# Turning keys, queries and normalised tiles by the DMA crossbar instead of TensorE, on a queue shared with stores

## The chip, the cores and the metric

One core of one Trainium2 chip. The metric is device microseconds (us) of one execution; a number for a kernel is the median of all its runs, slow ones included, with the lowest and highest beside it. An execution counts as fast or slow by its granted TensorE clock and its time; the ratios and their intervals use fast runs alone. The sets of experiments ran on different chips, each with the kernel before beside it.

## The reference, cut to what matters

Attention in chunks of 32 queries over their own keys, 16 to the left, 8 to the right and 8 memory rows, for 4 batches of 8 heads, 768 tokens, head size 64. Its output x (768 x 512 per batch) is normalised, multiplied by g, and goes through two large products with a ReLU between:

```python
for c in range(nc):                                   # 24 chunks of 32
    k_full = np.concatenate([mem_k, k[:, :, l_start:r_end]], axis=2)
    v_full = np.concatenate([mem_v, v[:, :, l_start:r_end]], axis=2)
    scores = scale * np.matmul(q_c, k_full.transpose(0, 1, 3, 2))
    a = np.exp(scores - max); a = a / (a.sum() + 1e-9)
    out[:, :, c_start:c_end] = np.matmul(a, v_full)
# x = out as (batch, 768, 512)
xn = (x - mu) / np.sqrt(var + 1e-06) * g_ln
return x + np.maximum(xn @ w_ch1, 0.0) @ w_ch2        # 512 -> 2048 -> 512
```

## The kernel before: the parts concerned

24 tiles of 128 tokens are worked in 8 units of three. A unit has 28 steps: 16 of the up-product (`up`, L319), then 12 of the down-product (`down`, L336). A table says at which step what else is put between: attention of the next unit's tiles, loads, and the turning of keys and queries. Every engine and every queue runs its own list in order.

```python
def turn_x(u, i, t, kind="att"):              # a normalised tile, 128 x 512, turned on TensorE
    pv = as16(slot("att")[:, 0, :]) ...
    for dt in range(4):
        nc.tensor.matmul(out=pv[...], lhsT=xn[t % 3][...], rhs=identity, is_transpose=True, ...)   # L296
    nc.scalar.copy(out=xT[u % 2][:, :, 128 * i : 128 * i + 128], in_=...)
# turn_kq (L176): 16 matmuls for a pair of heads of keys or queries; keep_k, keep_q copy them to KT, QZ
def v_around(b):                              # borders between groups of V, SBUF to SBUF, queue SP
    nc.sync.dma_start(out=vt[8:24, 1:NG, :, :], in_=vt[72:88, 0 : NG - 1, :, :])
    nc.sync.dma_start(out=vt[88:96, 0 : NG - 1, :, :], in_=vt[24:32, 1:NG, :, :])
...
elif u in (2, 4):
    attend(((1, 8, 8, 12), (4, 8, 10, 14), (11, 17, 17, 21)))   # scores, values, norm, turn_x of 3 tiles
    for j, step in ((0, 17), (2, 23)):
        at(step, kq_block, b, j, 0, NG, "mm"); at(step, keep_rest)
    for h in range(H):
        at(2 + 2 * h, load_v_head, b, h)
    at(21, mem_cols, b); at(21, v_mem, b); at(22, v_around, b)
elif following:
    attend(((12, 17, 17, 21), (14, 17, 17, 22), (18, 23, 23, 26)))
```

The softmax here doesn't subtract the row's maximum and nothing guards it: scores larger than these inputs give would overflow.

Of the kernel before, what the change touches and what calls it, by code (L numbers as in the profile page):

```python
# [9 lines left out]
FP16 = mybir.dt.float16  # L10
# [5 lines left out]
def kernel(  # L16
# [17 lines left out]
    KR = 96  # L34
    KC = NG * KR + 32
    HD = 65
# [21 lines left out]
    w2c = [sb.tile([128, 4, 512], FP16, name=f"w2c{i}") for i in range(4)]  # L58
    k16 = [sb.tile([96, H, 8, 64], FP16, name=f"k16_{i}") for i in range(2)]
    q16 = [sb.tile([96, H, 8, 64], FP16, name=f"q16_{i}") for i in range(2)]  # L60
    V = [sb.tile([128, NG, H, HD], FP16, name=f"V{i}") for i in range(2)]
    KT = [sb.tile([128, 4, KC], FP16, name=f"KT{i}") for i in range(2)]
    QZ = [sb.tile([128, 4, NG, 2, 64], FP16, name=f"QZ{i}") for i in range(2)]
    AT = [sb.tile([128, 2, H, 64], FP16, name=f"AT{i}") for i in range(3)]
# [45 lines left out]
    def load_v_group(b, g):  # L110

        lo, hi = max(64 * g - 16, 0), min(64 * g + 72, S)
        r = 24 + lo - 64 * g
        nc.gpsimd.dma_start(  # L114
            out=V[b % 2][r : r + hi - lo, g, :, 0:64],
            in_=dram(v, b * H * HS + lo * D, [[64, hi - lo], [HS, H], [1, 64]]),
        )

    def load_v_head(b, h):
        nc.gpsimd.dma_start(  # L120
            out=V[b % 2][24:88, :, h, 0:64],
            in_=dram(v, (b * H + h) * HS, [[64, 64], [64 * 64, NG], [1, 64]]),
        )

    def v_around(b):

        vt = V[b % 2]
        nc.sync.dma_start(out=vt[8:24, 1:NG, :, :], in_=vt[72:88, 0 : NG - 1, :, :])
        nc.sync.dma_start(out=vt[88:96, 0 : NG - 1, :, :], in_=vt[24:32, 1:NG, :, :])

    def v_mem(b):
        src = memv16[:, b, :, :]
        nc.sync.dma_start(
            out=V[b % 2][0:8, :, :, :],
            in_=bass.AP(tensor=src.tensor, offset=src.offset,
                        ap=[list(src.ap[0]), [0, NG], [1, H * HD]]),
        )
# [26 lines left out]
    def mem_cols(b):  # L164
        src = memKT[:, 4 * b : 4 * b + 4, :]
        nc.vector.tensor_copy(
            out=free(KT[b % 2], 0, [[KC, 4], [KR, NG], [1, 8]]),
            in_=bass.AP(tensor=src.tensor, offset=src.offset,
                        ap=[list(src.ap[0]), [8, 4], [0, NG], [1, 8]]),
        )  # L170
# [13 lines left out]
    def keep_k(pv, b, j, n, g0, g1, copy=nc.vector.tensor_copy):  # L184

        for ga, gb in ((0, 1), (1, NG - 1), (NG - 1, NG)):
            ga, gb = max(ga, g0), min(gb, g1)
            if ga < gb:
                lo = 0 if ga == 0 else 8 * ga - 2
                m = 10 if gb == NG else 8 * ga + 9 - lo  # L190
                copy(  # L191
                    out=free(KT[b % 2], j * KC + 24 + 32 * ga + 8 * lo,
                             [[KR, gb - ga], [8, m], [1, 8]]),
                    in_=free(pv, lo, [[8, gb - ga], [1, m], [n, 8]]),
                )

    def keep_q(copy, pv, b, j, par, n, g0, g1):


        rows = slice(64 * par, 64 * par + 64)  # L200
        copy(  # L201
            out=free(QZ[b % 2][rows, j, g0, par, :], 0, [[128, g1 - g0], [8, 8], [1, 8]]),
            in_=free(pv[rows, :], 8 * g0, [[8, g1 - g0], [1, 8], [n, 8]]),
        )
# [24 lines left out]
    def keep_rest():  # L229
        kept_later.pop(0)()  # L230

    def scores(b, t):
        p = slot("att")
        a = AT[t % 3]
        for gg in range(2):
            g = 2 * t + gg
            for j in range(4):
                nc.tensor.matmul(  # L238
                    out=p[:, gg, 128 * j : 128 * j + 128],
                    lhsT=KT[b % 2][:, j, KR * g : KR * g + 128],  # L240
                    rhs=QZ[b % 2][:, j, g, :, :],
                    start=True, stop=True,
                )
# [48 lines left out]

    def turn_x(u, i, t, kind="att"):
        pv = as16(slot("att")[:, 0, :]) if kind == "att" else as16(slot("mm")[:, :])
        for dt in range(4):
# [72 lines left out]
    def clear_k(i):  # L368
        nc.vector.memset(KT[i][:, :, 8:24], 0.0)
        nc.vector.memset(KT[i][:, :, NG * KR - 8 : KC], 0.0)  # L370

# [32 lines left out]
    for h in (0, 4):  # L404
        for which in range(2):
            load_kq(0, which, 0, CUT, h, h + 4)
    keep(counts[:, 0:1], counts[:, 0:1], 24, 0.0)
    keep(counts[:, 1:2], counts[:, 1:2], -88, 0.0)
    make_identity(nc, identity)
# [7 lines left out]
    mem_cols(0)  # L417
    pg = slot("mm")[:, :]
    nc.tensor.matmul(out=pg, lhsT=ones32, rhs=g_one, start=True, stop=True)
    nc.scalar.copy(out=g_row, in_=pg)  # L420
    v_mem(0)
# [5 lines left out]
    nc.gpsimd.memset(zero2[:, 1:2], -NEG)  # L427
    keep(band[:, 0:1], zero2[:, 0:1], -64, NEG)
    keep(band[:, 1:2], zero2[:, 0:1], 40, NEG)
    keep(zero2[:, 1:2], zero2[:, 1:2], -8, 0.0)  # L430
    nc.gpsimd.tensor_tensor(out=band[:, 1:2], in0=band[:, 1:2], in1=zero2[:, 1:2], op=ALU.add)
    for g in range(4, 6):
# [47 lines left out]
    scores(0, 1)  # L480
    stay_busy(5)
    values(0, 0)
# [20 lines left out]
    for u, tiles in enumerate(units):  # L503
# [6 lines left out]

        def attend(steps):

            for i, (s0, s1, s2, s3) in enumerate(steps):
                t = following[i]
                at(s0, scores, t // 6, t % 6)
                at(s1, values, t // 6, t % 6)
                at(s2, norm, t % 6, t % 9)
                at(s3, turn_x, u + 1, i, t % 6)
                at(min(s3 + 1, 27), root, t % 6, t % 9)

        late = ((16, 19, 19, 22), (17, 21, 21, 24), (19, 23, 23, 26))
        if u == 0:
# [10 lines left out]
            for g in range(6):  # L533
                at(15, load_v_group, 1, g)
            attend(late)
            at(26, mem_cols, 1)
            at(26, v_mem, 1)
        elif u == 1:
# [3 lines left out]
            for g in range(6, NG):  # L542
                at(0, load_v_group, 1, g)
            for which in range(2):
                at(1, load_kq, 2, which)
            attend(late)
        elif u in (2, 4):
            attend(((1, 8, 8, 12), (4, 8, 10, 14), (11, 17, 17, 21)))
            b = u // 2 + 1
            for j, step in ((0, 17), (2, 23)):  # L550
                at(step, kq_block, b, j, 0, NG, "mm")
                at(step, keep_rest)
            for h in range(H):
                at(2 + 2 * h, load_v_head, b, h)
            at(21, mem_cols, b)
            at(21, v_mem, b)
            at(22, v_around, b)
        elif following:
            attend(((12, 17, 17, 21), (14, 17, 17, 22), (18, 23, 23, 26)))
            if u == 3:  # L560
                for which in range(2):
                    at(2 + which, load_kq, 3, which)
        for step in range(16 + 4 * n):
# [43 lines left out]
```

## Time and profile before

| | before |
|---|---|
| time, beside the changed kernel's first run | 232.52 us (230.87 to 233.24, 4 runs) |
| span of the profiled run | 230.2 us |
| TensorE busy | 222.8 us, 97% of the span |
| waits of TensorE after 50 us | none listed |
| unit 2, unit 3 | 27.11 us, 24.04 us, TensorE busy throughout |

The lines, and what follows from them, are in the prediction.

### The profile page before, as it was taken

Reading aid. Unit: us, or ns where it says so; the run is one execution under the profiler, and the core shown is the slowest. Engines: PE = TensorE matmul, PEld = TensorE weight load, DVE = VectorE, ACT = ScalarE, POOL = GpSimd, SP = SyncE. Lnnn points to the kernel's source line nnn. Section 1 sums busy time; section 2 is a strip of 40 time slices with the busy share of each in tenths; the row PEclk is TensorE's granted clock in tenths of the full one; section 3 lists DMA queues with packets and bytes.
Section 4 is the critical chain, followed back from the end, with each engine's and each line's share of the span. In section 5 each row is a group of like instructions: output and inputs, shape, how many; then the busy total and the mean of one; then the engine's idle time right before and its main releaser. Section 6 shows DMA issues by size and latency. Waiting matters only on the chain.

```text
span 230.2 us, 5499 instructions
## 1 busy us (share of the span) xinstructions
PE 222.8 (97%) x2289; PEld 138.2 (60%) x2289; DVE 125.4 (54%) x290; ACT 119.0 (52%) x228; POOL 68.6 (30%) x125
## 2 busy tenths in 40 slices
PE   7989999899999999999999999999999999999993
PEld 2455776447765577555765577556765566557553
DVE  5746881475747639575336648674436542663222
ACT  3565648253894576655355367654356335534200
POOL 6973343877360380530001370410001200030000
PEclk9999999999999999999999999999999999999999
DMA  5999999999999999548921199543001200111012
GB/s 80 169 90 203 201 211 150 125 200 226 121 69 126 226 145 36 37 77 119 236 48 48 48 127 23 37 99 106 0 3 46 90 4 0 47 48 46 0 48 93
DMA packets 50307, 21.91 MB, mean 95 GB/s; under 512 B 37817, under 2 KB 46777, under 8 KB 50234
## 3 DMA queue, kind: packets, MB, share of 16 engines
q0 software_dynamic: 45680, 14.23, 90.1%
q1 hardware_dynamic: 4602, 7.33, 10.5%
q8 instruction: 18, 0.29, 0.6%
q14 instruction: 7, 0.06, 0.1%
HBM read 28.48 MB, written 6.29 MB: 151 GB/s over the span
## 4 chain that ended last, share of the span: by engine, by line
PE 77%; DMA 16%; POOL 2%; DVE 2%; issue 1%; POOLq 0%
PE mm L319 32%; PE mm L336 32%; DMA w2c<-in_moe_w_ch_dram 13%; PE att L238 4%; DMA V<-in_v_dram 3%; PE att L258 3%; PE att L176 3%; PE att L296 2%; POOL V L114 2%; PE mm L354 2%; PE mm L176 1%; DVE QZ L374 1%; DVE V L379 0%; DVE V L378 0%; DVE osb L359 0%
## 5 line engine op out<-in xcount | busy, mean ns | idle before, releaser
L319 PE MATMUL mm<-xT,w1c 128*128 128x384 f16 x512 | 88.3, 326 | 0.0
L336 PE MATMUL mm<-w2c,rT 128*128 128x512 f16 x368 | 87.4, 379 | 0.2 <-DMA w2c<-in_moe_w_ch_dram 0.2
L319 PEld LDWEIGHTS <-w1c 128*128 128x128 f16 x512 | 57.0, 114 | 24.2 <-issue 0.3
L327 DVE TENSOR_SCALAR rT<-mm 128x384 f16<-128x384 f32 x64 | 35.5, 556 | 35.3 <-PE mm L319 35.1
L336 PEld LDWEIGHTS <-rT 128*128 128x128 f16 x368 | 33.8, 98 | 34.0 <-issue 0.3
L325 ACT ACTIVATE rT<-mm 128x384 f16<-128x384 f32 x64 | 31.2, 489 | 35.9 <-PE mm L319 33.9
L245 ACT ACTIVATE AT<-att,band 96x512 f16<-96x512 f32 x48 | 30.1, 677 | 17.1 <-PE att L238 16.6
L287 POOL TENSOR_SCALAR veps<-squares 128x1 f32<-128x1 f32 x24 | 4.5, 188 | 109.9 <-ACT junk L284 95.1
L343 DVE SCALAR_TENSOR_TENSOR osb<-mm,rstd,xs 128x512 f32<-128x512 f32 x23 | 17.2, 749 | 30.9 <-PE mm L336 20.4
L114 POOL DMA_DIRECT2D V<-in_v_dram x24 | 21.5, 900 | 15.5 <-DMA V<-in_v_dram 4.5
L301 ACT COPY xT<-att 128x512 f16<-128x512 f16 x21 | 12.2, 581 | 23.8 <-PE att L296 23.8
L191 DVE COPY KT<-att 128x80 f16<-128x80 f16 (+3 forms) x44 | 18.4, 480 | 2.1 <-PE att L176 2.1
L278 DVE SCALAR_TENSOR_TENSOR xn<-xs,nmean,g_row 128x512 f16<-128x512 f32 x24 | 18.0, 752 | 0.9
L201 ACT COPY QZ<-mm 64x768 f16<-64x768 f16 (+1 forms) x18 | 13.6, 757 | 8.0 <-PE mm L176 7.8
L268 DVE RECIPROCAL rec<-att 128x8 f32<-128x8 f32 x24 | 4.9, 203 | 23.3 <-PE att L258 23.3
L284 ACT ACTIVATE junk<-xs,nmean 128x512 f16<-128x512 f32 x24 | 17.4, 724 | 0.1
L269 DVE SCALAR_TENSOR_TENSOR xs<-att,rec 128x512 f32<-128x512 f32 x24 | 16.6, 691 | 0.8
L238 PE MATMUL att<-QZ,KT 128*128 128x128 f16 x192 | 14.8, 219 | 0.9 <-ACT AT L245 0.6
L238 PEld LDWEIGHTS <-KT 128*128 128x128 f16 x192 | 12.6, 98 | 4.6 <-issue 1.4
L201 ACT COPY QZ<-att 64x384 f16<-64x384 f16 (+1 forms) x20 | 12.0, 598 | 5.3 <-PE att L176 5.1
L291 POOL TENSOR_TENSOR rstd<-veps,mhalf 128x1 f32<-128x1 f32 x24 | 13.3, 553 | 2.0
L258 PEld LDWEIGHTS <-AT 96*64 96x64 f16 x384 | 7.9, 111 | 8.7 <-issue 6.0
(63 smaller groups left out, 145.5 us busy)
## 6 DMA issues: line engine op xcount, KB each, us to landing
out_dram<-osb SPq DMA_DIRECT2D x23, 256.0 KB, 5.9
w1c<-in_moe_w_ch_dram POOLq DMA_DIRECT2D x4, 512.0 KB, 12.0
w2c<-in_moe_w_ch_dram POOLq DMA_DIRECT2D x4, 512.0 KB, 15.7
V<-in_v_dram POOLq DMA_DIRECT2D x20, 88.0 KB, 14.1
k<-in_k_dram POOLq DMA_DIRECT2D x2, 768.0 KB, 12.4
q<-in_q_dram POOLq DMA_DIRECT2D x2, 768.0 KB, 16.1
V<-in_v_dram POOLq DMA_DIRECT2D x16, 96.0 KB, 5.9
k<-in_k_dram POOLq DMA_DIRECT2D x3, 256.0 KB, 6.3
```

Source lines behind the costliest of these rows:

```text
L114: nc.gpsimd.dma_start(out=V[b % 2][r : r + hi - lo, g, :, 0:64], in_=dram(v, b * H * HS + lo * D, [[64, hi - lo], [HS, H], [1, 64]]),)
L191: copy(out=free(KT[b % 2], j * KC + 24 + 32 * ga + 8 * lo, [[KR, gb - ga], [8, m], [1, 8]]), in_=free(pv, lo, [[8, gb - ga], [1, m], [n, 8]]),
L201: copy(out=free(QZ[b % 2][rows, j, g0, par, :], 0, [[128, g1 - g0], [8, 8], [1, 8]]), in_=free(pv[rows, :], 8 * g0, [[8, g1 - g0], [1, 8], ...
L238: nc.tensor.matmul(out=p[:, gg, 128 * j : 128 * j + 128], lhsT=KT[b % 2][:, j, KR * g : KR * g + 128], rhs=QZ[b % 2][:, j, g, :, :], start ...
L245: nc.scalar.activation(out=free(a, 32 * c, [[512, 2], [64, 8], [1, 32]], KR), in_=free(p, 32 * c, [[512, 2], [64, 8], [1, 32]], KR), func= ...
L278: nc.vector.scalar_tensor_tensor(out=xn[i], in0=x, scalar=nmean[i], in1=g_row, op0=ALU.add, op1=ALU.mult,)
L284: nc.scalar.activation(out=junk, in_=xs[xi], func=ACTF.Square, bias=nmean[i], accum_out=squares[i],)
L319: nc.tensor.matmul(out=p, lhsT=free(w, i, [[4, 128]]), rhs=xT[u % 2][:, dt, 0 : 128 * n], start=(dt == 0), stop=(dt == 3),)
L325: nc.scalar.activation(out=o, in_=p, func=ACTF.Relu)
L327: nc.vector.tensor_scalar(out=o, in0=p, scalar1=0.0, scalar2=None, op0=ALU.max)
L336: nc.tensor.matmul(out=p, lhsT=rT[hc][:, 128 * i : 128 * i + 128], rhs=w2c[hc // 4][:, hc % 4, :], start=(hc == 0), stop=(hc == 15),)
L343: nc.vector.scalar_tensor_tensor(out=o, in0=p, scalar=rstd[t % 9], in1=xs[t % 9], op0=ALU.mult, op1=ALU.add,)
```

## The change

The intent: take the turning off TensorE. Keys and queries of batches 2 and 3 are loaded token by token and turned by the DMA crossbar in four parts each, fitted between the stores on SP's queue; VectorE spreads the queries over zeros; GpSimd copies the borders between key groups. 17 normalised tiles are turned by the crossbar as well. The product that spreads g over 128 rows moves behind the first scores, and the fillers around it (matmuls on zeros that keep TensorE busy, `stay_busy`) are exchanged. The steps of the attention of units 2 to 6 move too, as the diff shows. The layout of KT, QZ and V changes to suit. Core of the diff:

```diff
+    def load_tokens(b, which, t):              # six of each per batch, 256-byte runs
+        nc.gpsimd.dma_start(out=free(dst, 512 * t, [[64, H], [1, 64]]), in_=dram(src, ...))
+    def cross_k(b, half, t0, t1):
+        nc.sync.dma_start_transpose(out=free(KT[b % 2], ...), in_=kraw[0][64 * half : 64 * half + 64, 512 * t0 : 512 * t1])
+    def cross_q(half, t0, t1): ...             # the same into QT
+    def k_around(b, t0, t1): ...               # 4 GpSimd copies of key borders
+    def spread_q(b, half, t0, t1): ...         # 2 VectorE copies QT -> QZ
     def turn_x(u, i, t, kind="att"):
+        if kind == "dma":
+            nc.sync.dma_start_transpose(out=xT[u % 2][:, :, 128 * i : 128 * i + 128], in_=xn[t % 3])
+            return
...
-            for which in range(2):
-                at(1, load_kq, 2, which)
-            attend(late)
+            for t in range(6):
+                for which in range(2):
+                    at(23, load_tokens, 2, which, t)
+            attend(((16, 19, 19, 19), (17, 19, 20, 20), (21, 23, 23, 26)), "att")
...
+            if u in (3, 5):
+                attend(((10, 15, 15, 15), (12, 15, 16, 16), (17, 21, 21, 21)))
+            else:
+                attend(((9, 14, 14, 14), (11, 14, 15, 15), (16, 20, 20, 20)))
             if u in (2, 4):
-                kq_block ... at steps 17 and 23; v_mem at 21; v_around at 22
+                at(16, cross_k, b, 0, 0, 4)
+                at(20, cross_k, b, 1, 0, 4)
+                at(20, cross_q, 0, 0, 3)
+                at(21, cross_q, 1, 0, 3)
+                at(27, k_around, b, 0, 4)
+            elif u in (3, 5):
+                for half in range(2):
+                    at(6 + half, spread_q, b, half, 0, 3)
+                    at(1, cross_k, b, half, 4, 6)
+                    at(1, cross_q, half, 3, 6)
+                at(4, k_around, b, 4, 6)
+                at(5, v_mem, b)
+                at(5, v_around, b)
+                ... spread_q of the other half at 18 and 19
```

Line numbers move with it: L319 becomes L374, L336 L391, the values product L258 becomes L308; L345 is the crossbar transpose of a tile, L247 and L253 those of keys and queries, L130 and L131 the moves of V's borders, L401 the stores.

More of the change, by code (lines that the diff above doesn't have):

```diff
@@ L34 @@
     KR = 96
-    KC = NG * KR + 32
     HD = 65
@@ L58 @@
     w2c = [sb.tile([128, 4, 512], FP16, name=f"w2c{i}") for i in range(4)]
-    k16 = [sb.tile([96, H, 8, 64], FP16, name=f"k16_{i}") for i in range(2)]
-    q16 = [sb.tile([96, H, 8, 64], FP16, name=f"q16_{i}") for i in range(2)]
+    kraw = [sb.tile([128, 4096], FP16, name=f"kraw{i}") for i in range(2)]
+    qraw = [sb.tile([128, 4096], FP16, name=f"qraw{i}") for i in range(2)]
+    QT = sb.tile([128, NG * 4 * 64], FP16, name="QT")
+    k16 = [t[0:96, 0:4096].rearrange("p (h r d) -> p h r d", h=H, r=8) for t in kraw]
+    q16 = [t[0:96, 0:4096].rearrange("p (h r d) -> p h r d", h=H, r=8) for t in qraw]
     V = [sb.tile([128, NG, H, HD], FP16, name=f"V{i}") for i in range(2)]
-    KT = [sb.tile([128, 4, KC], FP16, name=f"KT{i}") for i in range(2)]
-    QZ = [sb.tile([128, 4, NG, 2, 64], FP16, name=f"QZ{i}") for i in range(2)]
+    KT = [sb.tile([128, NG * 4 * KR + 32], FP16, name=f"KT{i}") for i in range(2)]
+    QZ = [sb.tile([128, NG, 4, 2, 64], FP16, name=f"QZ{i}") for i in range(2)]
     AT = [sb.tile([128, 2, H, 64], FP16, name=f"AT{i}") for i in range(3)]
@@ L112, in load_v_group @@
         lo, hi = max(64 * g - 16, 0), min(64 * g + 72, S)
-        r = 24 + lo - 64 * g
+        r = 16 + lo - 64 * g
         nc.gpsimd.dma_start(
@@ L120, in load_v_head @@
         nc.gpsimd.dma_start(
-            out=V[b % 2][24:88, :, h, 0:64],
+            out=V[b % 2][16:80, :, h, 0:64],
             in_=dram(v, (b * H + h) * HS, [[64, 64], [64 * 64, NG], [1, 64]]),
@@ L127, in v_around @@
         vt = V[b % 2]
-        nc.sync.dma_start(out=vt[8:24, 1:NG, :, :], in_=vt[72:88, 0 : NG - 1, :, :])
-        nc.sync.dma_start(out=vt[88:96, 0 : NG - 1, :, :], in_=vt[24:32, 1:NG, :, :])
+        nc.sync.dma_start(out=vt[0:16, 1:NG, :, :], in_=vt[64:80, 0 : NG - 1, :, :])
+        nc.sync.dma_start(out=vt[80:88, 0 : NG - 1, :, :], in_=vt[16:24, 1:NG, :, :])
     def v_mem(b):
@@ L133, in v_mem @@
         nc.sync.dma_start(
-            out=V[b % 2][0:8, :, :, :],
+            out=V[b % 2][88:96, :, :, :],
             in_=bass.AP(tensor=src.tensor, offset=src.offset,
@@ L166, in mem_cols @@
         nc.vector.tensor_copy(
-            out=free(KT[b % 2], 0, [[KC, 4], [KR, NG], [1, 8]]),
+            out=free(KT[b % 2], KR - 8, [[KR, 4], [4 * KR, NG], [1, 8]]),
             in_=bass.AP(tensor=src.tensor, offset=src.offset,
@@ L191, in keep_k @@
                 copy(
-                    out=free(KT[b % 2], j * KC + 24 + 32 * ga + 8 * lo,
-                             [[KR, gb - ga], [8, m], [1, 8]]),
+                    out=free(KT[b % 2], (4 * ga + j) * KR + 16 + 8 * (lo - 8 * ga),
+                             [[4 * KR, gb - ga], [8, m], [1, 8]]),
                     in_=free(pv, lo, [[8, gb - ga], [1, m], [n, 8]]),
@@ L201, in keep_q @@
         copy(
-            out=free(QZ[b % 2][rows, j, g0, par, :], 0, [[128, g1 - g0], [8, 8], [1, 8]]),
+            out=free(QZ[b % 2][rows, g0, j, par, :], 0, [[512, g1 - g0], [8, 8], [1, 8]]),
             in_=free(pv[rows, :], 8 * g0, [[8, g1 - g0], [1, 8], [n, 8]]),
@@ L230, in keep_rest, with place, cross_q, k_around @@
         kept_later.pop(0)()
+    def place(b, g):
+        return g if b < 2 else g % 2 * (NG // 2) + g // 2
+    def load_tokens(b, which, t):
+        dst, src = ((kraw[0], k), (qraw[0], q))[which]
+        nc.gpsimd.dma_start(
+            out=free(dst, 512 * t, [[64, H], [1, 64]]),
+            in_=dram(src, b * H * HS + 128 * t * D, [[D, 128], [HS, H], [1, 64]]),
+        )
+    def cross_k(b, half, t0, t1):
+        nc.sync.dma_start_transpose(
+            out=free(KT[b % 2], (24 * half + 4 * t0) * KR + 16, [[KR, 4 * (t1 - t0)], [1, 64]]),
+            in_=kraw[0][64 * half : 64 * half + 64, 512 * t0 : 512 * t1],
+        )
+    def cross_q(half, t0, t1):
+        nc.sync.dma_start_transpose(
+            out=free(QT, (24 * half + 4 * t0) * 64, [[64, 4 * (t1 - t0)], [1, 64]]),
+            in_=qraw[0][64 * half : 64 * half + 64, 512 * t0 : 512 * t1],
+        )
+    def k_around(b, t0, t1):
+        kt, a = KT[b % 2], max(t0, 1)
+        own = lambda half, t: (24 * half + 4 * t) * KR
+        for dst, src, m, w in (
+            (own(1, t0), own(0, t0) + 64, t1 - t0, 16),
+            (own(0, a), own(1, a - 1) + 64, t1 - a, 16),
+            (own(0, t0) + 80, own(1, t0) + 16, t1 - t0, 8),
+            (own(1, a - 1) + 80, own(0, a) + 16, t1 - a, 8),
+        ):
+            nc.gpsimd.tensor_copy(
+                out=free(kt, dst, [[KR, 4 * m], [1, w]]), in_=free(kt, src, [[KR, 4 * m], [1, w]])
+            )
+    def spread_q(b, half, t0, t1):
+        for par in range(2):
+            rows = slice(64 * par, 64 * par + 64)
+            nc.vector.tensor_copy(
+                out=QZ[b % 2][rows, 6 * half + t0 : 6 * half + t1, :, par, :],
+                in_=QT[rows, (24 * half + 4 * t0) * 64 : (24 * half + 4 * t1) * 64].rearrange(
+                    "p (t j x) -> p t j x", j=4, x=64),
+            )
     def scores(b, t):
@@ L235, in scores @@
         for gg in range(2):
-            g = 2 * t + gg
+            g = place(b, 2 * t + gg)
             for j in range(4):
@@ L239, in scores @@
                     out=p[:, gg, 128 * j : 128 * j + 128],
-                    lhsT=KT[b % 2][:, j, KR * g : KR * g + 128],
-                    rhs=QZ[b % 2][:, j, g, :, :],
+                    lhsT=KT[b % 2][:, (4 * g + j) * KR : (4 * g + j) * KR + 128],
+                    rhs=QZ[b % 2][:, g, j, :, :],
                     start=True, stop=True,
@@ L293, in turn_x @@
     def turn_x(u, i, t, kind="att"):
+        if kind == "dma":
+            nc.sync.dma_start_transpose(
+                out=xT[u % 2][:, :, 128 * i : 128 * i + 128], in_=xn[t % 3]
+            )
+            return
         pv = as16(slot("att")[:, 0, :]) if kind == "att" else as16(slot("mm")[:, :])
@@ L368, in clear_k @@
     def clear_k(i):
-        nc.vector.memset(KT[i][:, :, 8:24], 0.0)
-        nc.vector.memset(KT[i][:, :, NG * KR - 8 : KC], 0.0)
+        end = 4 * KR * (NG - 1)
+        nc.vector.memset(free(KT[i], 0, [[KR, 4], [1, 16]]), 0.0)
+        nc.vector.memset(free(KT[i], end + 80, [[KR, 4], [1, 8]]), 0.0)
+        nc.vector.memset(KT[i][:, end + 4 * KR : end + 4 * KR + 32], 0.0)
     def clear_q(i, par):
@@ L406 @@
             load_kq(0, which, 0, CUT, h, h + 4)
-    keep(counts[:, 0:1], counts[:, 0:1], 24, 0.0)
-    keep(counts[:, 1:2], counts[:, 1:2], -88, 0.0)
+    keep(counts[:, 0:1], counts[:, 0:1], 16, 0.0)
+    keep(counts[:, 1:2], counts[:, 1:2], -80, 0.0)
     make_identity(nc, identity)
@@ L417 @@
     mem_cols(0)
-    pg = slot("mm")[:, :]
-    nc.tensor.matmul(out=pg, lhsT=ones32, rhs=g_one, start=True, stop=True)
-    nc.scalar.copy(out=g_row, in_=pg)
+    stay_busy(4)
     v_mem(0)
@@ L427 @@
     nc.gpsimd.memset(zero2[:, 1:2], -NEG)
-    keep(band[:, 0:1], zero2[:, 0:1], -64, NEG)
-    keep(band[:, 1:2], zero2[:, 0:1], 40, NEG)
-    keep(zero2[:, 1:2], zero2[:, 1:2], -8, 0.0)
-    nc.gpsimd.tensor_tensor(out=band[:, 1:2], in0=band[:, 1:2], in1=zero2[:, 1:2], op=ALU.add)
+    keep(band[:, 0:1], zero2[:, 0:1], -56, NEG)
+    keep(band[:, 1:2], zero2[:, 0:1], 32, NEG)
+    keep(zero2[:, 1:2], zero2[:, 1:2], 88, 0.0)
+    nc.gpsimd.tensor_tensor(out=band[:, 0:1], in0=band[:, 0:1], in1=zero2[:, 1:2], op=ALU.add)
     for g in range(4, 6):
@@ L480 @@
     scores(0, 1)
-    stay_busy(5)
+    stay_busy(2)
+    pg = slot("mm")[:, :]
+    nc.tensor.matmul(out=pg, lhsT=ones32, rhs=g_one, start=True, stop=True)
+    nc.vector.tensor_copy(out=g_row, in_=pg)
+    stay_busy(1)
     values(0, 0)
@@ L509, in at, with attend @@
             plan.setdefault(step, []).append((fn, args))
-        def attend(steps):
+        def attend(steps, kind="dma"):
             for i, (s0, s1, s2, s3) in enumerate(steps):
@@ L517, in attend @@
                 at(s2, norm, t % 6, t % 9)
-                at(s3, turn_x, u + 1, i, t % 6)
-                at(min(s3 + 1, 27), root, t % 6, t % 9)
-        late = ((16, 19, 19, 22), (17, 21, 21, 24), (19, 23, 23, 26))
+                at(s3, turn_x, u + 1, i, t % 6, kind if i == 2 or u == 0 else "dma")
+                at(min(s3 + 3, 27), root, t % 6, t % 9)
         if u == 0:
@@ L534 @@
                 at(15, load_v_group, 1, g)
-            attend(late)
+            attend(((16, 19, 19, 22), (17, 21, 21, 24), (19, 23, 23, 26)), "att")
             at(26, mem_cols, 1)
@@ L543 @@
                 at(0, load_v_group, 1, g)
-            for which in range(2):
-                at(1, load_kq, 2, which)
-            attend(late)
-        elif u in (2, 4):
-            attend(((1, 8, 8, 12), (4, 8, 10, 14), (11, 17, 17, 21)))
-            b = u // 2 + 1
-            for j, step in ((0, 17), (2, 23)):
-                at(step, kq_block, b, j, 0, NG, "mm")
-                at(step, keep_rest)
-            for h in range(H):
-                at(2 + 2 * h, load_v_head, b, h)
-            at(21, mem_cols, b)
-            at(21, v_mem, b)
-            at(22, v_around, b)
-        elif following:
-            attend(((12, 17, 17, 21), (14, 17, 17, 22), (18, 23, 23, 26)))
+            for t in range(6):
+                for which in range(2):
+                    at(23, load_tokens, 2, which, t)
+            attend(((16, 19, 19, 19), (17, 19, 20, 20), (21, 23, 23, 26)), "att")
+        elif following:
+            if u in (3, 5):
+                attend(((10, 15, 15, 15), (12, 15, 16, 16), (17, 21, 21, 21)))
+            else:
+                attend(((9, 14, 14, 14), (11, 14, 15, 15), (16, 20, 20, 20)))
+            b = u // 2 + 1
+            if u in (2, 4):
+                for h in range(H):
+                    at(2 + 2 * h, load_v_head, b, h)
+                at(16, cross_k, b, 0, 0, 4)
+                at(20, cross_k, b, 1, 0, 4)
+                at(20, cross_q, 0, 0, 3)
+                at(21, cross_q, 1, 0, 3)
+                at(21, mem_cols, b)
+                at(27, k_around, b, 0, 4)
[7 more added lines that the diff above has]
+                at(5, v_around, b)
+                for half in range(2):
+                    at(18 + half, spread_q, b, half, 3, 6)
             if u == 3:
-                for which in range(2):
-                    at(2 + which, load_kq, 3, which)
+                for t in range(6):
+                    for which in range(2):
+                        at(21, load_tokens, 3, which, t)
         for step in range(16 + 4 * n):
```

## The prediction

> **What bounds the kernel now.** I read the page's first two parts, then the waits of TensorE alone, then the chain that ended last, then the groups by shape. First the shares of the span and the slices:
>
> ```profile
> span 230.2 us, 5499 instructions
> PE 222.8 (97%) x2289; PEld 138.2 (60%) x2289; DVE 125.4 (54%) x290; ACT 119.0 (52%) x228; POOL 68.6 (30%) x125
> ...
> PE   7989999899999999999999999999999999999993
> ...
> PEclk9999999999999999999999999999999999999999
> DMA  5999999999999999548921199543001200111012
> ```
>
> TensorE (PE) is busy 97% of the span at the full granted clock; VectorE and ScalarE a little over half. The DMA row matters later: nearly full for the first 16 slices (92 us), then with holes. Asked for TensorE's waits from 50 us on, the trace lists none; in the whole run the waits inside the work (after the start) are at most 0.8 us, the last on a weight transfer at 48.9 us. So from 50 to 226 us each microsecond taken from TensorE is a microsecond of time, as long as nothing makes it wait. The chain says which pieces those are. A stretch of it, columns start, us and what:
>
> ```profile
> 94.63 0.68 PE att L176 x32
> 95.32 0.68 PE mm L176 x32
> 96.00 3.56 PE mm L336 x16
> 99.56 0.22 PE att L296 x4
> 99.78 1.73 PE mm L336 x8
> 101.50 0.80 PE att L176 x32
> 102.31 0.68 PE mm L176 x32
> 102.99 3.56 PE mm L336 x16
> 106.55 8.45 PE mm L319 x52
> ```
>
> L176 turns keys and queries of batch 2 on TensorE (128 small matmuls), L296 turns a normalised tile, L336 and L319 are the two big products. Both kinds of turning are on the chain. The evictions belonging to them:
>
> ```profile
> L201 ACT COPY QZ<-mm 64x768 f16<-64x768 f16 x16 | 12.7, 793 | 7.1 <-PE mm L176 7.0
> L191 DVE COPY KT<-att 128x880 f16<-128x880 f16 x12 | 12.8, 1064 | 0.0
> L301 ACT COPY xT<-att 128x512 f16<-128x512 f16 x21 | 12.2, 581 | 23.8 <-PE att L296 23.8
> out_dram<-osb SPq DMA_DIRECT2D x23, 256.0 KB, 5.9
> memk<-in_mem_k_dram SPq DMA_DIRECT2D x1, 64.0 KB, 1.9
> ```
>
> The first three have idle engines around them and cost no time now. The last two are the only landing times on the queue (SP) that the new transposes will use.
>
> **What the Trainium skill says.** "VectorE: DVE Perf Modes", section "The three transpose paths": 128x128 bf16 takes 390 ns on TensorE and 1309 ns by the DMA crossbar, which writes SBUF directly. The trace shows 219 ns for one L296 matmul, but four in 0.22 us of the chain, that is 55 ns of TensorE time each: pipelined, turning here is far cheaper than the page's single figure, so little is won per tile. "Advanced Engine Details and Errata", section "X-Bar Transpose (TRN2)": transposing DMAs are as fast as ordinary ones; the trace before has none, so it can't say. "VectorE: DVE Perf Modes", section "The TRN2 errata" gives 58 + elements/speed-up cycles at 0.96 GHz for SBUF to SBUF; no such f16 copy of size is in the trace, so I use it for an estimate of the new query copies only.
>
> **The change part by part.**
> 1. Keys and queries of batches 2 and 3 leave TensorE. From the chain: batch 2 loses 0.68 + 0.68 + 0.80 + 0.68 = 2.84 us, batch 3 (at 145.79, 146.47, 152.66, 153.46 us) the same 2.84. Sum 5.68 us, all on the path.
> 2. Normalised tiles turned by DMA: i = 0 and 1 of the unit after u = 1, and all three in u = 2 to 6, 17 tiles of 68 matmuls. Their pieces in the chain are 0.22 us, but for two of 0.35; 15 x 0.22 + 2 x 0.355 = 4.0 us, on the path. The listing of the instructions agrees: TensorE has 644 rows fewer, that is 2 x (256 + 68) less 4 for two more fillers.
> 3. Evictions that go: 16 ScalarE copies of 0.79 us, 17 of 0.58 us, and on VectorE 8 x (1.064 + 0.23 + 0.225) = 12.2 us. None is on the path, so they are worth nothing by themselves; they take away reasons to wait.
> 4. Added on VectorE: 16 copies spreading queries, 64 partitions x 768. Estimate by the skill's formula at four elements a cycle (58 + 192)/0.96 = 0.26 us each, 4 us in all. On GpSimd: 24 loads in place of 4 (about 0.75 us to issue, as the row of the head loads of V, 742 ns median), and 16 copies of key borders. Beside TensorE, with more than a unit between load and use in most places.
> 5. The product with g goes from 5.86 us to behind the first scores, with fillers exchanged. Before, its two passes took 1.36 us and four fillers now stand there; later 5 fillers become 3 and the product. This start is followed by waits for transfers (0.83 us for V at 44 us, 0.18 us for w2 at 48.9 us) that are set by the load queue, which hardly changes. I count 0 for it, half a microsecond either way.
> 6. Layout (memory rows last, groups outermost in KT and QZ): same sizes of matmuls, 0.
>
> Gross: 5.68 + 4.0 = 9.7 us, 4.2%.
>
> **What is given back.** The new dependence is a transposed tile needed whole at the next unit's first product. In units 2, 4 and 6 the last tile's values product is in step 20, so steps 21 to 27 remain, 7 x 0.866 (four L336 matmuls) = 6.1 us. From the end of the values product to xn the timeline of before shows 126.81 to 129.09 = 2.3 us (reciprocal, product, mean, L278). Left for issue, transpose and landing: 3.8 us. In units 3 and 5 step 21 is used, so 5.2 - 2.3 = 2.9 us. What does a 128 KB transpose take? Estimate: between the 64 KB load (1.9 us) and the 256 KB store (5.9 us) by a straight line, 1.9 + 64 x 4.0/192 = 3.2 us. That fits into even units and misses in odd ones by 0.3 to 0.7 us, with issue. In unit 3 the loads of batch 3's tokens run on the same 16 engines just then: I add 1 us. In unit 1 the third tile stays on TensorE, so no wait there. Sum 0.7 x 2 + 1 = about 2.4 us.
>
> Net 9.7 - 2.4 = 7.3 us; 232.9 - 7.3 = 225.6, and I say **225.3 us**.
>
> **The rivals.**
> *A. Nothing is given back.* The crossbar lands in 2 us or so (the skill's 1309 ns and "as fast as regular" point there, and the differing steps 20 and 21 look tuned). Then 232.9 - 9.7 = 223.2 us.
> *B. The tile transpose takes the place of the TensorE one as a wait.* If it lands only after 5.9 us, as the stores do, even units wait 2.1 us and odd ones 3.0: 3 x 2.1 + 2 x 3.0 = 12.3 us, more than the gain, 235.5 us. For it: all 23 stores have such a landing; against it: they write to DRAM and twice the bytes.
> *C. The SP queue is the bound.* Stores and transposes share one in-order queue, where each issue waits for its VectorE result. In units 3 and 5 four key and query transposes, then the fill of V's memory rows and the two moves of V's borders (0.73, 0.57, 1.0 us to issue before) stand in front of the values product of step 15, some 11 us into the unit. If one transpose costs SP 2 us to issue, 1 + 8 + 2.3 + landing 3 = 14 us, and TensorE waits 3 us twice: 229 to 231 us. Nothing in the trace of before measures that issue; the plain ones take 0.33 to 1.0 us, which speaks against 2.
> *D. VectorE or ScalarE becomes the bound.* Both lose more than they get; I give it next to nothing.
>
> **Range and chances.** A gives 223.2, the sum above 225.6, C about 230, B 235.5. I weigh A with 0.3, the sum with 0.4, C with 0.2 and B with 0.1. The 2% line is 228.3 us, beyond which C and B lie in part. Range 222.0 to 230.5 us; faster 0.76, same 0.20, slower 0.04.
>
> **What would show it.** Right: TensorE busy about 213 us, 324 turning matmuls gone from L176 and L296's successors, span near 222.5, no wait of TensorE over 1 us after 50 us except at unit starts, where the up-product waits for the DMA of xT, in units 4 and 6 first (after the odd ones). Step 1 wrong: TensorE's busy time falls by less than 9 us. Landing estimate wrong: transposes of xn landing well under 3 us (A) or near 6 us with a wait at every unit start (B). C: the values product at step 15 waiting for a DMA of V, and SP busy issuing. The prediction fails above all if the transposes, mixed with 256-byte token loads, land late, which would show as waits on DMA of KT, QT or xT.

## The result and the profile after

244.34 us (241.79 to 245.91, 4 runs, one of them slow) against 232.52 us: ratio 1.0482, interval 1.0374 to 1.0591. A ratio here is the mean time of one kernel's fast runs over that of the other's of the same rounds, so not quite the ratio of the medians quoted. The changed kernel is slower, outside the range.

The page's head and slices of the changed kernel:

```profile
span 242.3 us, 4931 instructions
PE 218.3 (90%) x1967; PEld 130.7 (54%) x1967; DVE 122.2 (50%) x285; ACT 98.6 (41%) x194; POOL 91.0 (38%) x161
...
PE   7989999899999999759679699989719999999995
...
PEclk9999999999999999989979999999977999999999
```

TensorE's busy time fell by 4.5 us only, its share to 90%, and there are slices at 1 to 7 tenths (each is 6.06 us) at 97 to 109, 115 to 127, 133 to 139 and 170 to 182 us. The clock row dips below 9 at or behind most of them. The timeline of TensorE names the waits (start, duration, group, and in brackets the idle time before and what ended it):

```profile
105.61 8.99 PE L374 MATMUL mm<-xT,w1c 128*128 128x384 f16 x44 [4.03 <-DMA xT<-xn]
...
122.59 0.71 PE L308 MATMUL att<-V,AT 96*64 96x65 f16 x32 [3.85 <-DMA V<-V]
...
138.44 6.66 PE L374 MATMUL mm<-xT,w1c 128*128 128x384 f16 x40 [2.06 <-DMA xT<-xn]
...
162.98 7.31 PE L374 MATMUL mm<-xT,w1c 128*128 128x384 f16 x44 [1.02 <-DMA xT<-xn]
...
180.95 1.10 PE L308 MATMUL att<-V,AT 96*64 96x65 f16 x32 [6.52 <-DMA V<-V]
```

Those are five waits, 17.5 us: three for a turned tile xT at a unit's start (4.03, 2.06, 1.02 us) and two for the moves of V's borders before the values product of step 15 in units 3 and 5 (3.85 and 6.52 us). No wait for KT or QT.

They cost more than themselves. Windows of the changed kernel, unit by unit: length, then busy TensorE, weight load, VectorE, ScalarE, GpSimd (number of instructions), granted clock, transfer share (the packets' time as a share of the 16 DMA engines'; above 1 where packets overlap), GB/s. Units 3, 5 and 6 do the same work on TensorE:

```profile
105.61:138.44 32.83, 26.92 (x185) 15.13 (x185) 14.69 (x34) 9.81 (x20) 10.75 (x20) 0.90 0.72 105
138.44:162.98 24.54, 23.52 (x185) 14.05 (x185) 12.14 (x27) 9.95 (x20) 12.58 (x21) 1.00 2.90 130
162.98:194.92 31.94, 25.42 (x185) 14.81 (x184) 13.87 (x33) 9.81 (x20) 4.04 (x13) 0.89 0.50 97
194.92:218.28 23.36, 23.36 (x186) 14.04 (x185) 11.86 (x26) 9.95 (x20) 2.21 (x6) 1.00 0.17 52
```

Unit 6, undisturbed, needs 23.36 us of TensorE; unit 3 needed 26.92 and unit 5 25.42 at mean clocks of 0.90 and 0.89. So 3.56 + 2.06 = 5.6 us went into matmuls at a lowered clock: in finer windows the clock reads 0.50 from 107 to 109 us, from 124 to 126 and from 181 to 185, each time shortly after one of the three long waits. The account: -9.7 (work removed) + 17.5 + 5.6 = 13.4, against 242.3 - 230.2 = 12.1; unit 2 began 1.38 us earlier than before, 0.44 us of it being two turned tiles, which the 9.7 already holds. The other 0.94, of which 0.54 came before unit 1 (begun at 51.19 us against 51.73), makes up most of the rest.

What SP's queue did in units 2 and 3 of the changed kernel (start, time held, instruction):

```profile
94.58 3.51 SPq L247 DMA_TRANSPOSE KT<-kraw  x1
...
98.83 3.91 SPq L345 DMA_TRANSPOSE xT<-xn  x1
...
104.27 3.37 SPq L253 DMA_TRANSPOSE QT<-qraw  x2
107.74 1.14 SPq L401 DMA_DIRECT2D out_dram<-osb  x2
108.98 1.93 SPq L247 DMA_TRANSPOSE KT<-kraw  x1
111.08 1.22 SPq L253 DMA_TRANSPOSE QT<-qraw  x1
112.35 1.52 SPq L247 DMA_TRANSPOSE KT<-kraw  x1
113.92 1.29 SPq L253 DMA_TRANSPOSE QT<-qraw  x1
...
116.95 1.06 SPq L131 DMA_DIRECT2D V<-V  x1
```

The third tile's transpose (98.83) held the queue for 3.91 us behind a key transpose. Another key and two query transposes, then two stores whose results VectorE had had ready since 99.1 and 102.4 us (its L398), then four more transposes until 115.21, stand before the moves of V, which were meant for step 5 and were issued at 116.3 to 118.0 us; the values product began at 122.59. And the landing times in the list of transfers:

```profile
out_dram<-osb SPq DMA_DIRECT2D x23, 256.0 KB, 2.3
...
xT<-xn SPq DMA_TRANSPOSE x17, 2.4
...
KT<-kraw SPq DMA_TRANSPOSE x8, 4.2
```

The list gives a tile 2.4 us at the median, sooner than the 3.2 us estimated, but the profile resolves only 3 of the 17 landings, and the tiles that TensorE waited for are mostly not among them. The tile issued at 133.11 us landed 5.28 us later (in the chain), and the wait for the one issued at 98.83 ended at 105.61. Loads were in flight beside both: beside the first the token loads of batch 3, issued from 131.1 us on; beside the second batch 2's eight loads of V, issued at 87.6 to 92.8 us, which landed until 103.6 by the completion events of the trace. The question is what stands before and beside a tile.

### The profile page after: what moved, and what is told of

The parts are those of the page before. It is cut to its first block, busy times and chain, and to the rows that moved or that the text cites. A ratio compares the mean times of both kernels' runs of the same rounds, so it can differ in the third digit from the quotient of the medians.

```text
span 242.3 us, 4931 instructions
## 1 busy us (share of the span) xinstructions
PE 218.3 (90%) x1967; PEld 130.7 (54%) x1967; DVE 122.2 (50%) x285; ACT 98.6 (41%) x194; POOL 91.0 (38%) x161
## 4 chain that ended last, share of the span: by engine, by line
PE 37%; SPq 12%; DMA 11%; POOL 5%; issue 2%; DVE 1%; ACT 0%; DVEq 0%; ACTq 0%; POOLq 0%
PE mm L391 18%; PE mm L374 14%; DMA V<-V 5%; SPq L247 4%; SPq L253 3%; DMA xT<-xn 3%; DMA V<-in_v_dram 3%; POOL kraw L241 2%; PE att L308 2%; PE att L288 2%; SPq L345 2%; POOL qraw L241 2%; PE mm L409 1%; SPq L401 1%; POOL rstd L341 1%
## 5 line engine op out<-in xcount | busy, mean ns | idle before, releaser
L374 PE MATMUL mm<-xT,w1c 128*128 128x384 f16 x512 | 89.2, 330 | 7.1 <-DMA xT<-xn 7.1
L391 PE MATMUL mm<-w2c,rT 128*128 128x512 f16 x368 | 87.7, 389 | 0.0
L374 PEld LDWEIGHTS <-w1c 128*128 128x128 f16 x512 | 57.2, 114 | 34.0 <-issue 10.1
L391 PEld LDWEIGHTS <-rT 128*128 128x128 f16 x368 | 35.2, 100 | 38.6 <-issue 2.8
L398 DVE SCALAR_TENSOR_TENSOR osb<-mm,rstd,xs 128x512 f32<-128x512 f32 x23 | 17.3, 751 | 34.8 <-PE mm L391 30.3
L116 POOL DMA_DIRECT2D V<-in_v_dram x24 | 21.5, 897 | 13.0 <-DMA w1c<-in_moe_w_ch_dram 3.6
L308 PE MATMUL att<-V,AT 96*64 96x65 f16 x384 | 10.6, 201 | 11.9 <-DMA V<-V 10.4
L308 PEld LDWEIGHTS <-AT 96*64 96x64 f16 x384 | 8.4, 114 | 18.9 <-issue 14.9
L319 DVE SCALAR_TENSOR_TENSOR xs<-att,rec 128x512 f32<-128x512 f32 x24 | 16.6, 691 | 0.8
L288 PEld LDWEIGHTS <-KT 128*128 128x128 f16 x192 | 13.1, 100 | 4.9 <-issue 1.4
L288 PE MATMUL att<-QZ,KT 128*128 128x128 f16 x192 | 15.3, 223 | 0.2 <-DVE QZ L203 0.2
L268 POOL COPY KT<-KT 128x128 f16<-128x128 f16 (+4 forms) x16 | 4.3, 296 | 28.7 <-DMA KT<-kraw 28.7
L341 POOL TENSOR_TENSOR rstd<-veps,mhalf 128x1 f32<-128x1 f32 x24 | 13.4, 558 | 2.0
L122 POOL DMA_DIRECT2D V<-in_v_dram x16 | 11.9, 760 | 0.1
```

What stands on the lines that cost most here:

```text
L116: nc.gpsimd.dma_start(out=V[b % 2][r : r + hi - lo, g, :, 0:64], in_=dram(v, b * H * HS + lo * D, [[64, hi - lo], [HS, H], [1, 64]]),)
L288: nc.tensor.matmul(out=p[:, gg, 128 * j : 128 * j + 128], lhsT=KT[b % 2][:, (4 * g + j) * KR : (4 * g + j) * KR + 128], rhs=QZ[b % 2][:, g ...
L308: nc.tensor.matmul(out=p[64 * gg : 64 * gg + 64, h // 4, c0 : c0 + HD], lhsT=AT[t % 3][0:KR, gg, h, :], rhs=V[b % 2][0:KR, 2 * t + gg, h, ...
L319: nc.vector.scalar_tensor_tensor(out=x.rearrange("p (h d) -> p h d", h=H), in0=free(p, 0, [[128, H], [1, 64]]), scalar=1.0, in1=free(r, 0, ...
L374: nc.tensor.matmul(out=p, lhsT=free(w, i, [[4, 128]]), rhs=xT[u % 2][:, dt, 0 : 128 * n], start=(dt == 0), stop=(dt == 3),)
L391: nc.tensor.matmul(out=p, lhsT=rT[hc][:, 128 * i : 128 * i + 128], rhs=w2c[hc // 4][:, hc % 4, :], start=(hc == 0), stop=(hc == 15),)
```

## The experiments

Theory Q: the order on the one SP queue makes the waits (V's moves behind key and query transposes). Rivals: L, a tile transpose is simply too late for its deadline; T, the short runs of the token loads hold up the transposes; M, the moves of V are slow whatever queue they are on. All results below were judged correct (but see e4). The kernel before ran beside each: 231.97, 231.89, 231.06 and 231.29 us medians in the four sets.

### Tiles alone: e1_tiles_only

```diff
-   token loads, cross_k, cross_q, k_around, spread_q of batches 2, 3
+   load_kq of batch 2 at step 1 of unit 1, of batch 3 at steps 2 and 3 of unit 3; kq_block at steps 2 and 5, keep_rest 2 later
+   v_mem at 21, v_around at 22 of the even units (as before the change)
```

> Only the normalised tiles go through the crossbar (17 tiles, same steps as in the change); keys and queries of batches 2 and 3 are loaded and turned on TensorE as before, and V's borders are moved at steps 21 and 22 of the even units, ahead of need. Theory Q (the order on the one SP queue: key and query transposes hold up the moves of V's borders and the third tile's transpose): no wait of TensorE on V, waits on xT under 1 us in all, gain about the 4.0 us of the tiles: 228.5 to 230 us. Rival L (a tile transpose simply lands too late for its deadline): the waits on xT stay, 7 us or so, time 233 to 238 us.

Measured: 238.44 us (237.63 to 240.82), ratio 1.0304. One wait on xT, at the start of unit 2, and 2.5 us of waits of my own making (keys turned too close together). The chain of that run, start, duration, what:

```profile
73.58 10.61 DMA xT<-xn
```

The transposes that were issued at 71.85 to 74.8 us landed at 84.2. The long key and query loads of batch 2 had been issued at 66.2 and 67.2 us. Neither theory had foreseen this: a tile issued with only stores and another tile before it on its queue landed 10.6 us after its issue. The run is spoilt as a test of L, and missed both expectations, but gives the hint that loads in flight matter.

### Keys and queries alone: e2_keys_only

```diff
-   turn_x(..., "dma")
+   turn_x(..., "att"), four steps after the norm
```

> Only keys and queries of batches 2 and 3 go through the crossbar, at the steps of the change; all tiles are turned on TensorE. Theory Q: the SP queue reaches the moves of V's borders some 4 us earlier than in the change, since no tile transposes stand in front, so the waits on V shrink from 10.4 us to 1 to 6 us; no wait on xT; 228 to 234 us. Rival L: nothing is left of the loss, 227 us, because the late tiles caused it and delayed the rest.

Measured: 240.0 us (237.64 to 240.41), ratio 1.0317. TensorE's waits:

```profile
PE att L308 <- DMA V<-V: 10.8, 2, 5.5
```

No wait on xT, and V's stay whole: Q's 1 to 6 us was too little, and its 228 to 234 us was missed by 6. L, by which the late tiles delay the rest, falls: the waits on V need no tile.

### V's moves on another queue: e3_moves_on_act

```diff
-        nc.sync.dma_start(out=vt[0:16, 1:NG, :, :], ...)       # and the second move, and v_mem for b >= 2
+        nc.scalar.dma_start(out=vt[0:16, 1:NG, :, :], ...)
```

> The change, with only the fill of V's memory rows and the two border moves of batches 2 and 3 issued from ScalarE's queue instead of SP's, at the same step. Theory Q: they are issued 5 to 8 us earlier, the waits on V (10.4 us) go to under 2 us and with them the stretches at half clock behind them, about 3 us; waits on xT stay at 7 us: 230 to 233 us. Rival M (the moves are slow by themselves, or stand behind the transposes in the transfer engines whatever queue issues them): the waits on V stay over 6 us, 240 us or more.

Measured: 232.93 us (231.8 to 236.29), ratio 1.0017: 11 us less than the change, by the fast runs too, from the issuing queue of six transfers. The profile is of the one run counted as slow (236.29 us), so its waits are shown with that reserve. TensorE's waits:

```profile
PE mm L374 <- DMA xT<-xn: 6.4, 3, 3.9
PE att L308 <- DMA V<-V: 3.5, 2, 2.0
```

V's waits fall from 10.4 to 3.5 us (Q had said under 2), xT's stay, as Q says. M is right in part: from the last move's issue to the end of the wait the chain has 7.91 us in this run, beside transposes, and 5.51 us in the changed kernel. By these two figures the moves want to be issued some 6 to 8 us ahead.

### The tokens in long runs: e4_long_loads

```diff
-        nc.gpsimd.dma_start(out=free(dst, 512 * t, [[64, H], [1, 64]]), in_=dram(src, ...))   # six
+        if t == 0:
+            nc.gpsimd.dma_start(out=dst[:, 0:3072], in_=dram(src, b * H * HS, [[3072, 128], [1, 3072]]))
```

> The change, but keys and queries of a batch come in one load each with long contiguous runs in place of six loads with 256-byte runs. The tokens lie in wrong places, so the result is wrong on purpose; every transpose, copy and product is the same in size. Rival T (the short runs of the token loads fill the transfer engines and hold up the transposes): waits fall from 17.5 us to under 5 us, 225 to 230 us. Theory Q: the loads are long done when the transposes are issued; 240 us or more, the waits on V and xT stay at 12 us or more.

Measured: 249.36 us (247.12 to 249.91), ratio 1.0723; the wrong order of tokens passed the comparison, so this output is not a test of the tokens' places. T falls: without short runs it is slower still. Two tile transposes in its chain:

```profile
101.06 2.44 DMA xT<-xn
...
132.24 10.87 DMA xT<-xn
```

The first, its batch's token loads issued 24 us before (76.7 and 77.4 us), landed in 2.44 us. The second was issued 2 us after the two long loads of batch 3 (130.2 and 130.9 us) and took 10.87 us, with a wait of 7.65 us behind it. Not the length of the runs but a load in flight holds up a transpose.

### Only the place of V's moves: e8_moves_early

```diff
-                at(5, v_mem, b);  at(5, v_around, b)           # in the odd unit
+                at(22, v_mem, b); at(22, v_around, b)          # in the even unit, same SP queue
```

> The change with one edit: the fill and the moves of V's borders stand at step 22 of the even unit on the same SP queue instead of step 5 of the odd one. All tiles by the crossbar as in the change. Order theory: the 10.4 us of waits on V vanish with the half clock behind them (some 3 us); waits on xT stay at 6 to 7 us: 230 to 232 us.

Measured: 230.97 us (227.71 to 233.23), ratio 0.9902. Nothing but the place of three transfers per batch on the same queue has changed, and the time goes from 11.8 us above the kernel before to 0.9 below it: 12.7 us by the medians, some 13.5 us by the ratios of the fast runs (1.0482 and 0.9902). TensorE's list has no wait on V's moves; this is what is left:

```profile
PE mm L374 <- DMA xT<-xn: 5.6, 2, 3.5
```

### The third tile on TensorE: e5_moves_on_act_third_pe and e6_moves_early_third_pe

```diff
-                at(s3, turn_x, u + 1, i, t % 6, kind if i == 2 or u == 0 else "dma")
+                at(s3 + 4 if i == 2 and u > 1 else s3, turn_x, u + 1, i, t % 6, "att" if i == 2 or u == 0 else "dma")
```

The first is on top of e3, the second on top of e8.

> The change with the fill and border moves of V on ScalarE's queue and, in units 2 to 6, the third tile turned on TensorE four steps later, the first two still by the crossbar. If the two waits (on V, on the third tile's xT) are the whole loss besides the half clock that follows them, this keeps 9.7 - 5 x 0.22 = 8.6 us of the gain, less about 3 us of rest waits on V: 225 to 229 us, waits on xT none. If instead the transposes slow the work in some other way, it stays near 232 us.

> As the run before, but the moves of V stay on SP's queue and stand at step 22 of the even unit, behind the transposes of step 20 and 21 and before the four transposes of the next unit. Order theory: no wait on V at all, none on xT, 223 to 226 us, faster than both kernels. Rival (the crossbar is too slow for the key and query transposes at any place): waits then show on KT or QT in the odd units, scores of step 10 or the copies that spread queries, 228 us or more.

Measured: e5 230.48 us (227.16 to 232.91; two of four runs slow), ratio 0.9845; e6 225.42 us (224.36 to 226.93), ratio 0.9694. e5 missed its range and its "waits on xT none" (2.1 us). In its profile, a slow run of 232.91 us, ScalarE, held by issuing the moves, made TensorE wait 2.9 us for its ReLU; on two fast runs against four, the other queue is the worse cure. In e6 one wait is left, 2.0 us on xT at the end of unit 2, though the tile there was not the third:

```profile
94.28 10.51 DMA xT<-xn
```

### Why that tile is late: e11_first_cross_later and e9_loads_early

```diff
 # e11, on e6
-                at(16, cross_k, b, 0, 0, 4)
+                at(20, cross_k, b, 0, 0, 4)
 # e9, on e6
-                    at(23, load_tokens, 2, which, t)
+                    at(4, load_tokens, 2, which, t)
+   unit 1 turns all its tiles on TensorE; ScalarE's squares (root) are tied to the norm's step
```

> The same best kernel with one edit: the first key transpose of a batch at step 20 instead of 16, so nothing but a store follows the two tile transposes for 4 steps; loads as before. If the key transpose holds up the tiles in front of it, the 2.0 us wait on xT at the end of unit 2 goes, 222 us. If the loads do, it stays at 1 to 3 us, and the moves of V land 3 us later, still in time: 225 to 226 us.

> The best so far (V's moves at step 22, third tile on TensorE; 225.4 us), with batch 2's token loads at step 4 of unit 1 instead of step 23, so that they and V's loads end some 8 us earlier, and unit 1's tiles turned on TensorE (0.44 us) because those would meet the loads. What is left there is one wait of 2.0 us on xT at the end of unit 2, whose transposes were issued at 92.5 us and landed at 104.9, with the transfer share above 2 all along. If loads in flight beside a transpose hold it up, the wait and its 1.7 us of half clock go: 222.5 us, no wait on xT. If the key transpose behind it on the queue does, the wait stays: 226 us.

Measured: e11 225.36 us (223.89 to 225.48), ratio 0.9721; e9 223.51 us (222.9 to 226.03), ratio 0.9681. In e11 no transpose follows the two tiles for four steps, and the tile is as late as before:

```profile
92.59 10.39 DMA xT<-xn
```

In e9 the token loads are over by then and the last load of V lands at 96.9 us instead of 104.6 in e6 (completion events); the wait at the end of unit 2 is gone. Its one remaining wait is at the end of unit 4, beside batch 3's loads:

```profile
PE mm L374 <- DMA xT<-xn: 1.2, 1, 1.2
```

So what stands behind on the queue does not delay the tile; loads in flight do. That rests on the traces: the ratios of e6, e11 and e9 (0.9694, 0.9721, 0.9681) can't be told apart.

### Tiles alone, mended: e7_tiles_only_again

```diff
 # on e1
+   unit 1 turns all tiles on TensorE; kq_block at steps 17 and 23 as in the kernel before
```

> Tiles alone by the crossbar, mended: the first try met the long key and query loads of unit 1 (xT landed some 9 us after its issue) and had its own waits from keys turned too close together. Here unit 1 turns all tiles on TensorE and units 2 to 6 turn all three by the crossbar, keys and queries on TensorE at the steps of the kernel before. If the tile transposes are hurt only by what stands in front of them or moves beside them, no wait on xT over 0.5 us and a gain of 15 x 0.22 = 3.3 us plus two longer ones: 228 to 229 us. If a tile transpose is too slow for its deadline by itself, waits of 1 to 3 us in units 3 and 5.

Measured: 227.7 us (227.32 to 229.09), ratio 0.9819, interval 0.9766 to 0.9871 (unclear at 2%), clock 1.00, no wait on xT in the list. All fifteen tiles, third ones too, at the steps of the change, meet their deadline. L is refuted.

### The product with g alone: e12_g_only

```diff
 # on the kernel before
-    product with g behind mem_cols, copied by ScalarE ... stay_busy(5)
+    stay_busy(4) ... stay_busy(2), product with g, copied by VectorE, stay_busy(1)
```

> The kernel before with only the product with g moved behind the first scores and the fillers exchanged as in the change. Predicted worth 0, half a microsecond either way. Unit 1 began 0.54 us earlier in the change than before: if that is the move's doing, 231.4 us; if it is the spread of the load queue, 231.9 us and no clear difference.

Measured: 231.2 us (230.7 to 232.16, 6 runs), ratio 0.999, interval 0.9952 to 1.0029: no difference.

### The version that beats both: e13_best

```diff
 # on e9
-                        at(21, load_tokens, 3, which, t)
+                        at(5, load_tokens, 3, which, t)
+   third tiles of units 5 and 6 by the crossbar again, at the steps of the change
```

> The kernel with batch 2's loads early (223.5 us), with batch 3's token loads at step 5 of unit 3 instead of 21, and the third tile of units 5 and 6, beside which no load runs, by the crossbar again. If loads in flight are what holds up transposes, the last wait on xT (1.17 us at the end of unit 4) goes and the two thirds of units 5 and 6 land without a wait (they did in the change and in the tiles-only run): 223.5 - 1.2 - 0.4 = 222 us. If units 3's first two tiles, which now meet the loads, land over 10 us late, a wait on xT at the end of unit 3 of some 1 to 3 us shows instead, 224 us.

Measured: 222.79 us (221.49 to 224.1, 6 runs), ratio 0.9627, interval 0.958 to 0.9673. The head of its page:

```profile
span 221.0 us, 4957 instructions
PE 214.7 (97%) x1987; PEld 130.3 (59%) x1987; DVE 122.9 (56%) x285; ACT 101.0 (46%) x199; POOL 91.4 (41%) x161
```

TensorE is at 97% again and no wait of it after 50 us is listed. 8.5 us of the 9.7 are realised; the tiles that stay on TensorE are five more than in the change (1.1 us). Against e9 (interval 0.9615 to 0.9748) the gain in time is not clear of noise; the vanished wait is read from the trace.

## Why the prediction was wrong, point by point

- **Parts 1 and 2, work removed: right.** Unit 4 of the changed kernel, free of slow clock, has 23.52 us of TensorE where before it had 27.11: 3.59 us, against 2.84 + 0.80. Unit 6 has 0.69 us less, against 0.66. e7 and e13 turn it into time.
- **Part 3 and rival D: right.** VectorE and ScalarE were never the bound.
- **Part 4:** a query copy took 0.357 us, not 0.26; off the path. The prediction used the table's row alone: "VectorE: DVE Perf Modes", "The TRN2 errata", says below its table that this row under-predicts and that the measured fixed term is about 150 cycles, and an estimate from that, (150 + 192)/0.96 = 0.356 us, agrees with the trace. Nor was the trace before without an f16 copy from SBUF to SBUF: a smaller one, KT<-memKT, 128x384, took 278 ns where the row at four elements a cycle gives 160.
- **Part 5, g: right**, by e12. Part 6, layout, has no run of its own and stays untested.
- **"What is given back": this step failed.** It summed 2.4 us, all from the tile's deadline. Measured were 17.5 us of waits and 5.6 us of lowered clock. The waits on xT came at the starts of units 3, 4 and 5, the longest after the even unit 2, which was to have none. (From 225.6 to the 225.3 us forecast no step is given.) It failed in four terms:
  - *The landing of a tile.* Estimated 3.2 us. It is 2.4 us with the engines free, so neither odd nor even units would wait (e7); but 5.3 us (issued at 133.11) in the changed kernel and some 10.4 to 10.9 us (e1, e4, e6, e11) with loads in flight. I had added 1 us for loads, in unit 3 alone, and none for the loads of V in units 2 and 4. The 5.9 us of the stores, from which the 3.2 us and rival B came, was no property of all 23: the listing of the output tensor's instructions in the trace before reads `DMA to landing us min/median/max: 2.0/5.9/7.6`, from the four that the profile resolves: 7.6 us twice, beside loads (issued at 70.8 and 107.5 us), 4.2 and 2.0. By the completion events, of the nine stores issued from 120 to 183 us, after the loads in front of them had landed, eight took 2.0 us.
  - *The moves of V's borders.* They were in rival C only, at 6 us and a weight of 0.2, instead of in the sum. e8 shows them to be the largest single part: 12.7 us with the clock.
  - *The terms inside C.* Four transposes 8 us: they took 6.2 (108.98 to 115.21). Landing of the moves 3 us: 5.5. Start 1 us into the unit: 3.4, because the queue still held the last unit's transposes and stores. The sum of 14 us after the unit's start was 17.0 (105.61 to 122.59), and in unit 5 18.0 (162.98 to 180.95).
  - *The clock.* No step of the prediction let a wait cost more than its length.
- **Weights.** I took differing steps 20 and 21 as a sign of tuning and so gave A 0.3. That was an inference about the author, not from the profile; and B and C are not alternatives to the sum but further terms of it.
- The last paragraph did name what came to pass: the wait at step 15 for a DMA of V, SP busy issuing, and loads beside transposes. It was seen and mis-weighed.

What stays open: why a transpose beside loads lands so late. The runs show that it does, for short and long runs alike, and not by which mechanism. The completion events narrow it. In the eleven runs that have them, 158 tile transposes were issued: the 107 with no earlier load from GpSimd in flight completed 2.4 to 4.4 us after issue; of the 51 beside such loads, 49 completed only after the last of these loads had, 0.2 to 3.8 us behind it (in e11 the tile of 92.59 us at 102.98, the load at 102.79). No run moves the loads alone and leaves V's moves at step 5, so how much of the queue's lateness was itself the loads' doing (a tile held it 3.91 us beside loads, 1.19 us without) is not shown.

## What to carry to other kernels

When work moves from a full engine to an in-order transfer queue, write down that queue's whole list with issue times, and count for each transfer when its turn comes, not at which step it was put there; a transfer that something waits for goes in front of those that have time. Keep transposes away from loads in flight, and count a wait of some microseconds on TensorE together with the clock it costs. Here the same transfers cost 12 us in one order and gained 8.5 us in another, after moving three transfers per batch, the token loads, and five tiles.

## What the Trainium skill lacked or had wrong

- "Advanced Engine Details and Errata", "X-Bar Transpose (TRN2)", has transposing DMAs as fast as regular ones. Here a 128 x 512 f16 transpose (128 KB) held the issuing queue 1.19 us and up to 3.91, a 256 KB store 0.33; alone it landed 2.4 us after issue, a store of twice the bytes in 2.0. Beside loads both were late: the transpose took up to 10.9 us (e4), the store issued at 98.19 us in the changed kernel 7.0.
- "DMA: Bandwidth & Descriptors", "Rules for kernel authors", says that a transpose next to ordinary DMAs needs nothing. That is about correctness, against which no run here speaks; of time it says nothing, and a load in flight cost 8 us of landing (10.6 us in e1, 2.4 without).
- The same page, "Issuing engines are not separate DMA queues", says that issuing from several engines saves only the sequencer's time, usually small. Moving six transfers to ScalarE's queue took 11 us off the time (e3): on SP their turn came late.
- No page that I read gives a measured time for an SBUF to SBUF move over 16 and 8 partitions: 5.5 us from the issue of the second to the end of TensorE's wait, 179 and 89 KB, at a transfer share of 0.38 (118 to 122 us).
- "TensorE: Matmul & The Clock Gate", "Part 1: The HAM clock gate", asks for no idle gaps over about 3.4 us. The trace agrees for the waits of 3.85, 4.03 and 6.52 us (clock 0.50 after them); but waits of 2.02 us in e6 and 2.09 us in e8 were also followed by slow matmuls (the next 44 or 40 of L374 took 8.99 and 8.34 us), while 2.06 us in the changed kernel was not (6.66 us for 40).
